# Doubles of the output weights: converted beside the first maxout block instead of beside the experts

## The chip, the cores and the metric

The kernel runs on one core of one Trainium2 chip. The metric is the device time of one execution in microseconds (us). The core's engines are named as the profile names them: PE (matrix products; PEld are its weight loads), DVE (vector), ACT (scalar and activation), POOL, and SP, which here only issues transfers. Each engine takes its instructions in the order in which the program lists them.

## The reference

Three parts follow each other: a linear attention with a norm per head, a mixture of 8 experts (each of 2304 tokens goes to one of them), and a maxout layer with an output product.

```python
kv = einsum('bhsd,bhse->bhde', k, v); out = einsum('bhsd,bhde->bhse', q, kv)
x = out / sqrt(mean(out*out) + 1e-6) * g_norm          # 2304 tokens x 512
e = argmax(x @ w_gate)                                 # one of 8 experts per token, gate weight g
y = g * (maximum(x @ w1[e], 0) @ w2[e])                # w1 512x1024, w2 1024x512 per expert
h = maximum(maximum(y @ m1, y @ m2), y @ m3)           # m1, m2, m3: 512x768
result = h @ w_out                                     # w_out: 768x512
```

The four weights of the last two lines come as 64-bit doubles (`m2w1` to `m2w3` and `m2wo` in the kernel). The gate weight is applied after the output product.

## The kernel before

**Precision.** The engines have no 64-bit type, so a double is first made a float32, from its two 32-bit words: two activations scale the high and the low word (L912, L913), DVE shifts and masks (L914, L915, L917), POOL multiplies and adds (L918, L919). Each float32 weight is then split into a high and a low half that PE takes in its fast format: ACT copies the high half (L297), DVE subtracts for the low half (L298). Every product is three matmuls: high by high, high by low, low by high (`mm3`, L764 to L767).

**Stages.** The attention comes first (to about 88 us), then 8 experts (to about 337 us), then 6 maxout blocks of 384 tokens.

**Experts.** Expert r has an f loop of 8 steps (`gemm1_f`: 12 matmuls into ph, then h by ACT L788 and DVE L789) and a dc loop of 4 steps (`gemm2_dc`: 24 matmuls py, then y by ACT L801). The weights are one expert ahead: `split_next` makes tiles out of raw buffers (four of them, 512 KB each, loaded by SP), one tile per step of the f loop and two per step of the dc loop. In the same steps stand the rounds over the doubles: `DBL1[r]` lists the steps f, `DBL2[r]` the number per step dc. A round (`dbl_step`) stores what was converted three rounds ago to a DRAM tensor (a DMA issued by ACT, L924), loads a block three rounds ahead (SP, L899) and converts a block of 128x256 doubles. There are 48 of these: 36 for the three maxout weights, 12 for the output weights. The float32 results are read back from DRAM as raw buffers (L267, L270) and split.

**Maxout blocks.** Block j has 6 steps c. Each has 36 matmuls into three psum tiles pa (one per weight, out of six psum buffers), then ACT copies the first to m (L1096), DVE takes the maximum with the second and the third (L1097, L1098), ACT and DVE split the result into h2 (L1099, L1100). In block 0 a `split_next(2)` stands between the matmuls of a step and L1096. Then three groups of 18 matmuls pz (L1109 to L1111) form the output of 128 tokens each, over c = 0 to 5, and POOL scatters it by token number.

**What sets the order.** The schedule is manual: each engine's queue holds its instructions in the order of the program. So what is written ahead of L1096 is also ahead of it in ACT's queue. `spill` runs only if an expert has more tokens than its budget.

Of the kernel before, what the change touches and what calls it, by code (L numbers as in the profile page):

```python
# [9 lines left out]
F32 = mybir.dt.float32  # L10
F32R = mybir.dt.float32r
BF16 = mybir.dt.bfloat16
I32 = mybir.dt.int32
U32 = mybir.dt.uint32
ALU = mybir.AluOpType
AF = mybir.ActivationFunctionType
# [5 lines left out]
B, H, S, D = 4, 8, 576, 64  # L22
NT, DM, NE, FF, F2 = B * S, H * D, 8, 1024, 768
NDC, NFC, NC2 = DM // 128, FF // 128, F2 // 128
# [16 lines left out]
def kernel(  # L41
# [16 lines left out]
    nc = tc.nc  # L58
# [3 lines left out]
    xs = dram.tile([ZROW + 1, DM], I32, name="xs")  # L62
    ct = dram.tile([NT, 3], F32, name="ct")

    doubles = []
    if m2w1.dtype == mybir.dt.int64:
        d64 = [m2w1, m2w2, m2w3, m2wo]
        m2w1, m2w2, m2w3 = (dram.tile([DM, F2], F32, name=f"m2w{a}") for a in range(3))
        m2wo = dram.tile([F2, DM], F32, name="m2wo")
        for cb in range(F2 // 256):  # L70
            for a, dst in enumerate([m2w1, m2w2, m2w3]):
                for rb in range(NDC):
                    doubles.append((d64[a], dst, rb, cb))
        for rb in range(NC2):
            for cb in range(DM // 256):
                doubles.append((d64[3], m2wo, rb, cb))
    ND = len(doubles)
    m2w = [m2w1, m2w2, m2w3]

# [151 lines left out]


    sp, act = ENG.SP, ENG.Activation
    NRAW = NE * 8 + 12
    NW = 20
    NT1 = 16 * NE
    e_reg, raws, wt, wpools = {}, {}, {}, {}
# [2 lines left out]
    def wtile(i):  # L240
        if i < NT1:
            s = i % NW
        else:
            s = (i - NT1 + NT1 % NW) % NW if i - NT1 < NW else NW + i - NT1 - NW
        pool = wpools[0 if s < 4 else 1 if s < NW else 2]
        return pool.tile([128, 2, 4, 128], F32R, tag=f"w{s}", name=f"w{i}")

    def raw_dma(i):
        raw = rawp.tile([128, 1024], F32, tag="raw", name=f"raw{i}")
        raws[i] = raw  # L250
        if i < NE * 8:
            r, j = divmod(i, 8)
            if r not in e_reg:
                e_reg[r] = nc.values_load(er_i[0:1, r:r + 1] if r else e0_i[0:1, 0:1], engines=[sp],
                                          min_val=0, max_val=NE - 1)
            e = e_reg[r]
            if j < 4:
                src = w1[ds(e, 1), :, j * 256:(j + 1) * 256].rearrange("o (c p) f -> p (o c) f", p=128)
            else:
                dp_, hf = divmod(j - 4, 2)  # L260
                src = w2[ds(e, 1), hf * 512:(hf + 1) * 512, dp_ * 256:(dp_ + 1) * 256].rearrange(
                    "o (c p) f -> p (o c) f", p=128)
            return nc.sync.dma_start(raw.rearrange("p (c f) -> p c f", c=4), src)
        j = i - NE * 8
        if j < 9:
            a, cp = j % 3, j // 3
            return nc.sync.dma_start(raw.rearrange("p (c f) -> p c f", c=4),  # L267
                                     m2w[a][:, cp * 256:(cp + 1) * 256].rearrange("(c p) f -> p c f", p=128))
        j -= 9
        return nc.sync.dma_start(raw.rearrange("p (c f) -> p c f", c=2),  # L270
                                 m2wo[j * 256:(j + 1) * 256, :].rearrange("(c p) f -> p c f", p=128))

    stream, issued, ready = [0], [0], [8]

# [3 lines left out]
            raw_dma(issued[0])  # L278
            issued[0] += 1

    def split_next(n=1, eng=None):
        for _ in range(n):
            i, half = divmod(stream[0], 2)
            stream[0] += 1
            if i >= NRAW:
                continue
            raw = raws[i]
            t_ = wtile(2 * i + half)
            wt[2 * i + half] = t_
            if i < NE * 8 + 9:  # L290
                src = raw.rearrange("p (c f) -> p c f", c=4)[:, :, half * 128:(half + 1) * 128]
                hi, lo = t_[:, 0], t_[:, 1]
            else:
                src = raw[:, half * 512:(half + 1) * 512]
                hi = t_[:, 0].rearrange("p c f -> p (c f)")
                lo = t_[:, 1].rearrange("p c f -> p (c f)")
            nc.scalar.activation(out=hi, in_=src, func=AF.Copy)  # L297
            (eng or nc.vector).tensor_tensor(out=lo, in0=src, in1=hi.bitcast(F32), op=ALU.subtract)  # L298
            if half == 1:
                raw_upto(i + 5)  # L300

# [598 lines left out]
                              src[rb * 128:(rb + 1) * 128, cb * 256:(cb + 1) * 256].bitcast(I32))  # L900

    def dbl_round(i):

        if i < ND:
            t_ = dt_[i]
            w_ = dpool[0].tile([128, 256], F32, tag="dw", bufs=6, name=f"dw{i}")
            dt_[i, "w"] = w_
            lo, hi = t_[:, :, 0], t_[:, :, 1]  # L910
            wi = w_.bitcast(I32)
            nc.scalar.activation(out=w_, in_=hi.bitcast(F32), func=AF.Copy, scale=2.0 ** -112)  # L912
            nc.scalar.activation(out=lo.bitcast(F32), in_=lo.bitcast(U32), func=AF.Copy, scale=2.0 ** -52)  # L913
            nc.vector.tensor_scalar(out=wi, in0=wi, scalar1=3, scalar2=None, op0=ALU.logical_shift_left)  # L914
            nc.vector.scalar_tensor_tensor(out=wi, in0=hi, scalar=-2 ** 31, in1=wi,  # L915
                                           op0=ALU.bitwise_and, op1=ALU.bitwise_or)
            nc.vector.tensor_scalar(out=hi, in0=wi, scalar1=-2 ** 23, scalar2=None, op0=ALU.bitwise_and)  # L917
            nc.gpsimd.tensor_tensor(out=lo.bitcast(F32), in0=hi.bitcast(F32), in1=lo.bitcast(F32), op=ALU.mult)  # L918
            nc.gpsimd.tensor_tensor(out=w_, in0=lo.bitcast(F32), in1=w_, op=ALU.add)  # L919

    def dbl_store(i):
        if 0 <= i < ND:
# [103 lines left out]
    ct_gen, rk_gen = ct_compute(), ranking()  # L1026


    DBL1 = [(), (3, 5), (3, 5), (1, 3, 5), (1, 4), (1, 4), (1, 4), (1, 3, 5, 7)]
    DBL2 = [(0, 0, 0, 0), (1, 1, 1, 2), (1, 2, 1, 2), (1, 2, 1, 2), (1, 1, 1, 2)] + [(1, 1, 1, 1)] * 2 + [(2, 2, 0, 0)]  # L1030
    for r in range(NE):
        if r == 0:
            parts = [(0, RB[0], slice(0, RB[0]))]
# [48 lines left out]
    for j in range(NYB):  # L1082
        h2 = []
        for c in range(NC2):
            pa = [ps_tile(f"pa{j}{c}{a}") for a in range(3)]
            for a in range(3):
                w_ = m2t(a, c)
                for dc in range(NDC):
                    x_ = ysp[j, dc]
                    mm3(pa[a][:, :YB], w_[:, 0, dc], w_[:, 1, dc], x_[:, 0], x_[:, 1], dc == 0, dc == NDC - 1)  # L1090
            if j == 0:
                split_next(2)
            m_ = xgp.tile([128, H, D], F32, tag="xn", name=f"m{j}{c}").rearrange("p h d -> p (h d)")[:, :YB]
            t_ = hpool.tile([128, 2, YB], F32R, tag="h", name=f"g{j}{c}")
            h2.append(t_)
            nc.scalar.activation(out=m_, in_=pa[0][:, :YB], func=AF.Copy)  # L1096
            nc.vector.tensor_tensor(out=m_, in0=pa[1][:, :YB], in1=m_, op=ALU.max)  # L1097
            nc.vector.tensor_tensor(out=m_, in0=pa[2][:, :YB], in1=m_, op=ALU.max)  # L1098
            nc.scalar.activation(out=t_[:, 0], in_=m_, func=AF.Copy)  # L1099
            nc.vector.tensor_tensor(out=t_[:, 1], in0=m_, in1=t_[:, 0].bitcast(F32), op=ALU.subtract)  # L1100
        if j + 1 < NYB:
            ysplit(j + 1)
        for g in range(NG):
            jt = j * NG + g
            po = ps_tile(f"pz{jt}")
            for c in range(NC2):
                w_ = wot(c).rearrange("p s c f -> p s (c f)")
                h_ = h2[c][:, :, g * 128:(g + 1) * 128]
                nc.tensor.matmul(po, h_[:, 0], w_[:, 0], start=c == 0, stop=False)  # L1109
                nc.tensor.matmul(po, h_[:, 0], w_[:, 1], start=False, stop=False)  # L1110
                nc.tensor.matmul(po, h_[:, 1], w_[:, 0], start=False, stop=c == NC2 - 1)  # L1111
            o_ = xgp.tile([128, H, D], F32, tag="xn", name=f"o{jt}").rearrange("p h d -> p (h d)")
            nc.scalar.activation(out=o_, in_=po, func=AF.Copy, scale=ctab[:, jt, 1:2])  # L1113
            nc.gpsimd.indirect_dma_start(  # L1114
                out=out, out_offset=IndirectOffsetOnAxis(ap=ctab[:, jt, 0:1].bitcast(I32), axis=0),
                in_=o_, in_offset=None)
# [4 lines left out]
    with tc.If(flag):  # L1121
        spill(ctx, tc, dict(
            er_f=er_f, nr_f=nr_f, mr_f=mr_f, trir=trir, capf=capf, e2304=e2304, slot=slot, ident=ident, g2=g2,
            xs=xs, ct=ct, w1=w1, w2=w2, m2w=m2w, m2wo=m2wo, out=out))


def spill(ctx, tc, a):
# [3 lines left out]
    with ExitStack() as st:  # L1131
# [57 lines left out]
        for i in range(3):  # L1189
            nc.sync.dma_start(m2[i], a["m2w"][i].rearrange("(c p) f -> p c f", p=128))  # L1190
        wo = wpool.tile([128, NC2, DM], F32, name="sp_wo")
        nc.sync.dma_start(wo, a["m2wo"].rearrange("(c p) f -> p c f", p=128))

        def ps(nm):
            return psp.tile([128, 512], F32, tag="ps", name=nm)
# [100 lines left out]
```

## Time and profile before

| | before |
|---|---|
| time, median of 3 runs | 647.64 us (646.8 to 650.21) |
| profiled execution, own time | 650.49 us |
| its span (first to last instruction) | 648.6 us |
| mean granted clock of PE | 0.982 |
| PE busy | 619.0 us, 95% of the span |
| DVE busy | 338.0 us, 52% |
| ACT busy | 274.0 us, 42% |
| POOL busy | 196.5 us, 30% |
| bytes moved by DMA | 88.35 MB |

Busy times are unions of the instructions' spans, from one profiled execution, while the median comes from other runs. A busy share over the whole span mixes stages with different limits, so it has to be asked by stage. Matmuls overlap each other, so a busy PE is told best by the distance between the starts of two matmuls. In the rows, "idle before <-releaser" is the time that an engine stood and the instruction that ended it; "w<-raw" reads as "writes w, reads raw".

### The profile page before, as it was taken

Reading aid. Unit: us, or ns where it says so; the run is one execution under the profiler, and the core shown is the slowest. Engines: PE = TensorE matmul, PEld = TensorE weight load, DVE = VectorE, ACT = ScalarE, POOL = GpSimd, SP = SyncE. Lnnn points to the kernel's source line nnn. Section 1 sums busy time; section 2 is a strip of 40 time slices with the busy share of each in tenths; the row PEclk is TensorE's granted clock in tenths of the full one; section 3 lists DMA queues with packets and bytes.
Section 4 is the critical chain, followed back from the end, with each engine's and each line's share of the span. In section 5 each row is a group of like instructions: output and inputs, shape, how many; then the busy total and the mean of one; then the engine's idle time right before and its main releaser. Section 6 shows DMA issues by size and latency. Waiting matters only on the chain.

```text
span 648.6 us, 11278 instructions
## 1 busy us (share of the span) xinstructions
PE 619.0 (95%) x4113; PEld 593.8 (92%) x4113; DVE 338.0 (52%) x718; ACT 274.0 (42%) x629; POOL 196.5 (30%) x278
## 2 busy tenths in 40 slices
PE   8898988999999999999999999999999999999992
PEld 8788888999998989999999989989989989989992
DVE  2546867886889888888985322222322222221220
ACT  1655864856575857576753221121121121121110
POOL 3247643122858585857530010010010010001001
PEclk9978998999999999999999999999999999999997
DMA  8999347866888788888962000000000000000000
GB/s 226 282 297 297 122 164 236 256 234 214 246 249 276 235 264 254 259 251 255 275 184 65 1 34 16 1 33 17 1 33 17 0 17 33 0 17 33 1 18 35
DMA packets 81373, 88.35 MB, mean 136 GB/s; under 512 B 15017, under 2 KB 70825, under 8 KB 81314
## 3 DMA queue, kind: packets, MB, share of 16 engines
q1 hardware_dynamic: 68448, 66.64, 35.5%
q0 software_dynamic: 5952, 14.65, 6.5%
q10 hardware_dynamic: 6914, 6.30, 2.8%
q8 instruction: 34, 0.56, 0.4%
q14 instruction: 25, 0.20, 0.1%
HBM read 71.80 MB, written 15.76 MB: 135 GB/s over the span
## 4 chain that ended last, share of the span: by engine, by line
PE 63%; DVE 9%; DMA 4%; issue 3%; ACT 2%; ACTq 0%; POOL 0%; SPq 0%; DVEq 0%; POOLq 0%
PE pa L767 12%; PE pa L766 12%; PE pa L765 12%; PE py L766 4%; DVE w L298 4%; PE py L767 4%; PE py L765 4%; PE pz L1110 4%; PE pz L1109 4%; PE pz L1111 4%; DVE h L789 2%; DMA d<-in_moe_w_dram 2%; PE ph L767 2%; PE ph L766 2%; PE ph L765 2%
## 5 line engine op out<-in xcount | busy, mean ns | idle before, releaser
L766 PE MATMUL pa<-ys,w 128*128 128x384 f32 x432 | 144.3, 334 | 0.0
L765 PE MATMUL pa<-ys,w 128*128 128x384 f32 x432 | 144.3, 334 | 0.0
L767 PE MATMUL pa<-ys,w 128*128 128x384 f32 x432 | 144.3, 334 | 0.0
L298 DVE TENSOR_TENSOR w<-raw,w 128x512 fp32r<-128x512 f32 x152 | 114.6, 783 | 26.7 <-ACT w L297 23.1
L1114 POOL DMA_INDIRECT out_dram<-o,ctab x18 | 17.5, 973 | 286.9 <-ACT o L1113 276.7
L1097 DVE TENSOR_TENSOR m<-pa,m 128x384 f32<-128x384 f32 x36 | 20.1, 558 | 137.6 <-PE pa L767 137.6
L297 ACT ACTIVATE w<-raw 128x512 fp32r<-128x512 f32 x152 | 89.5, 624 | 4.8 <-DMA raw<-in_moe_w_dram 4.8
L766 PE MATMUL py<-h,w 128*128 128x324 f32 (+7 forms) x256 | 81.4, 318 | 7.2 <-DVE h L789 7.2
L1099 ACT ACTIVATE g<-m 128x384 fp32r<-128x384 f32 x36 | 18.9, 526 | 150.0 <-DVE m L1098 150.0
L766 PEld LDWEIGHTS pa<-ys,w 128*128 128x128 f32 x432 | 81.1, 188 | 0.2
L765 PEld LDWEIGHTS pa<-ys,w 128*128 128x128 f32 x432 | 81.1, 188 | 0.2
L767 PEld LDWEIGHTS pa<-ys,w 128*128 128x128 f32 x432 | 81.1, 188 | 0.0
L765 PE MATMUL py<-h,w 128*128 128x324 f32 (+7 forms) x256 | 80.2, 313 | 0.0
L767 PE MATMUL ph<-xt,w 128*128 128x324 f32 (+7 forms) x256 | 79.6, 311 | 0.5 <-DVE w L298 0.5
L765 PE MATMUL ph<-xt,w 128*128 128x324 f32 (+7 forms) x256 | 79.3, 310 | 0.6 <-ACT xt L667 0.6
L767 PE MATMUL py<-h,w 128*128 128x324 f32 (+7 forms) x256 | 79.8, 312 | 0.0
L766 PE MATMUL ph<-xt,w 128*128 128x324 f32 (+7 forms) x256 | 79.4, 310 | 0.2 <-DVE xt L668 0.2
L766 PEld LDWEIGHTS py<-h,w 128*128 128x128 f32 x256 | 48.8, 191 | 10.8 <-DVE h L789 10.6
L918 POOL TENSOR_TENSOR d<-d 128x256 f32<-128x256 f32 x48 | 30.7, 640 | 75.5 <-issue 18.2
L765 PEld LDWEIGHTS ph<-xt,w 128*128 128x128 f32 x256 | 48.3, 189 | 0.8 <-ACT xt L667 0.8
L767 PEld LDWEIGHTS ph<-xt,w 128*128 128x128 f32 x256 | 48.3, 189 | 0.8 <-DVE w L298 0.8
L765 PEld LDWEIGHTS py<-h,w 128*128 128x128 f32 x256 | 48.9, 191 | 0.0
(247 smaller groups left out, 1034.1 us busy)
## 6 DMA issues: line engine op xcount, KB each, us to landing
raw<-in_moe_w_dram SPq DMA_DIRECT2D x64, 512.0 KB, 5.4
d<-in_moe_w_dram SPq DMA_DIRECT2D x36, 256.0 KB, 5.2
m2w<-dw ACTq DMA_DIRECT2D x36, 128.0 KB, 4.5
raw<-m2w SPq DMA_DIRECT2D x9, 512.0 KB, 4.6
k<-in_k_dram SPq DMA_DIRECT2D x8, 512.0 KB, 8.7
v<-in_v_dram SPq DMA_DIRECT2D x8, 512.0 KB, 9.2
q<-in_q_dram SPq DMA_DIRECT2D x8, 512.0 KB, 8.5
d<-in_moe_w_out_dram SPq DMA_DIRECT2D x12, 256.0 KB, 5.2
```

The source lines that it names most:

```text
L297: nc.scalar.activation(out=hi, in_=src, func=AF.Copy)
L298: (eng or nc.vector).tensor_tensor(out=lo, in0=src, in1=hi.bitcast(F32), op=ALU.subtract)
L765: nc.tensor.matmul(po, lhi, rhi, start=first, stop=False)
L766: nc.tensor.matmul(po, lhi, rlo, start=False, stop=False)
L767: nc.tensor.matmul(po, llo, rhi, start=False, stop=last)
L918: nc.gpsimd.tensor_tensor(out=lo.bitcast(F32), in0=hi.bitcast(F32), in1=lo.bitcast(F32), op=ALU.mult)
L1097: nc.vector.tensor_tensor(out=m_, in0=pa[1][:, :YB], in1=m_, op=ALU.max)
L1099: nc.scalar.activation(out=t_[:, 0], in_=m_, func=AF.Copy)
L1109: nc.tensor.matmul(po, h_[:, 0], w_[:, 0], start=c == 0, stop=False)
L1110: nc.tensor.matmul(po, h_[:, 0], w_[:, 1], start=False, stop=False)
L1111: nc.tensor.matmul(po, h_[:, 1], w_[:, 0], start=False, stop=c == NC2 - 1)
L1114: nc.gpsimd.indirect_dma_start(out=out, out_offset=IndirectOffsetOnAxis(ap=ctab[:, jt, 0:1].bitcast(I32), axis=0), in_=o_, in_offset=None)
```

## The change

Only the 36 blocks of the three maxout weights stay in the rounds beside the experts. Their places in `DBL1` and `DBL2` are set anew: expert 1 to 7 had 7, 8, 9, 7, 6, 6 and 8 steps, and has 7, 8, 8, 6, 4, 3 and 3 (the last three steps only store). The output weights are loaded as doubles into the raw buffers (128 rows, 512 KB each, six of them), and `split_next` converts them in block 0 of the maxout stage, 128x512 at a time, into a tile of the pool from which m and the outputs come (tag xn, three buffers), and splits that into the weight tile. Step c = 0 still splits two tiles of a maxout weight; c = 1 converts two tiles, c = 2 to 5 one each. Both halves of each tile are also stored to DRAM (`m2wos`, 512 KB per tile, on SP's queue), where `spill` would read them. Gone are the float32 copy of the output weights in DRAM, its 12 stores and its three reloads. The conversion's seven instructions are the same, moved into a function.

```diff
-        d64 = [m2w1, m2w2, m2w3, m2wo]
+        d64 = [m2w1, m2w2, m2w3]
-        m2wo = dram.tile([F2, DM], F32, name="m2wo")
+        m2wos = dram.tile([F2, 2, DM], F32, name="m2wos")
-        for rb in range(NC2):
-            for cb in range(DM // 256):
-                doubles.append((d64[3], m2wo, rb, cb))
...
-    NRAW = NE * 8 + 12
+    NRAW = NE * 8 + 9 + NC2
...
-        return nc.sync.dma_start(raw.rearrange("p (c f) -> p c f", c=2),
-                                 m2wo[j * 256:(j + 1) * 256, :].rearrange("(c p) f -> p c f", p=128))
+        return nc.sync.dma_start(raw.bitcast(I32), m2wo[j * 128:(j + 1) * 128, :].bitcast(I32))
...
+    def to_float32(lo, hi, w_):
+        wi = w_.bitcast(I32)
+        nc.scalar.activation(out=w_, in_=hi.bitcast(F32), func=AF.Copy, scale=2.0 ** -112)
+        nc.scalar.activation(out=lo.bitcast(F32), in_=lo.bitcast(U32), func=AF.Copy, scale=2.0 ** -52)
+        nc.vector.tensor_scalar(out=wi, in0=wi, scalar1=3, scalar2=None, op0=ALU.logical_shift_left)
+        nc.vector.scalar_tensor_tensor(out=wi, in0=hi, scalar=-2 ** 31, in1=wi,
+                                       op0=ALU.bitwise_and, op1=ALU.bitwise_or)
+        nc.vector.tensor_scalar(out=hi, in0=wi, scalar1=-2 ** 23, scalar2=None, op0=ALU.bitwise_and)
+        nc.gpsimd.tensor_tensor(out=lo.bitcast(F32), in0=hi.bitcast(F32), in1=lo.bitcast(F32), op=ALU.mult)
+        nc.gpsimd.tensor_tensor(out=w_, in0=lo.bitcast(F32), in1=w_, op=ALU.add)
...
             else:
-                src = raw[:, half * 512:(half + 1) * 512]
-                hi = t_[:, 0].rearrange("p c f -> p (c f)")
-                lo = t_[:, 1].rearrange("p c f -> p (c f)")
+                half = 1
+                hi, lo = (t_[:, x].rearrange("p c f -> p (c f)") for x in range(2))
+                src = xgs[0].tile([128, H, D], F32, tag="xn", name=f"wd{i}").rearrange("p h d -> p (h d)")
+                words = raw.bitcast(I32).rearrange("p (f c) -> p f c", c=2)
+                to_float32(words[:, :, 0], words[:, :, 1], src)
             nc.scalar.activation(out=hi, in_=src, func=AF.Copy)
-            (eng or nc.vector).tensor_tensor(out=lo, in0=src, in1=hi.bitcast(F32), op=ALU.subtract)
+            nc.vector.tensor_tensor(out=lo, in0=src, in1=hi.bitcast(F32), op=ALU.subtract)
+            if i >= NE * 8 + 9:
+                c0 = (i - NE * 8 - 9) * 128
+                nc.sync.dma_start(m2wos[c0:c0 + 128].rearrange("p s f -> p (s f)"),
+                                  t_.bitcast(F32).rearrange("p s c f -> p (s c f)"))
             if half == 1:
                 raw_upto(i + 5)
...
-    DBL1 = [(), (3, 5), (3, 5), (1, 3, 5), (1, 4), (1, 4), (1, 4), (1, 3, 5, 7)]
-    DBL2 = [(0, 0, 0, 0), (1, 1, 1, 2), (1, 2, 1, 2), (1, 2, 1, 2), (1, 1, 1, 2)] + [(1, 1, 1, 1)] * 2 + [(2, 2, 0, 0)]
+    DBL1 = [(), (3, 5, 7), (1, 3, 5, 7), (1, 3, 5, 7), (3, 7), (7,), (), (1, 3, 5)]
+    DBL2 = [(0,) * 4] + [(1,) * 4] * 3 + [(1,) * 4, (1, 1, 1, 0), (1, 1, 1, 0), (0,) * 4]
...
             if j == 0:
-                split_next(2)
+                split_next(2 if c < 2 else 1)
```

## Rows read from the trace of the kernel before

**Rows 1.** Busy by stage: us, then PE, PEld, DVE, ACT, POOL, PEclk, DMA, GB/s.
```profile
215.00:245.00 30.00, 28.72 (x195) 27.95 (x193) 27.35 (x51) 19.67 (x47) 20.30 (x27) 1.00 0.81 253
337.00:387.00 50.00, 50.00 (x272) 47.65 (x272) 20.01 (x36) 15.81 (x32) 1.99 (x2) 1.00 0.10 33
```

**Rows 2.** PE's waits: waiting line, releaser, us in total, times, longest.
```profile
PE py L766 <- DVE h L789: 7.2, 13, 1.2
```

**Rows 3.** Timeline of PE, experts 0 and 7: start, us, instruction [idle before <-releaser].
```profile
107.81 0.42 PE L766 MATMUL py<-h,w 128*128 128x324 f32 x1 [1.16 <-DVE h L789]
...
109.42 0.54 PE L766 MATMUL py<-h,w 128*128 128x324 f32 x1 [0.90 <-DVE h L789]
...
325.21 0.30 PE L767 MATMUL py<-h,w 128*128 128x284 f32 x1
325.35 0.29 PE L765 MATMUL py<-h,w 128*128 128x284 f32 x1
325.83 0.40 PE L766 MATMUL py<-h,w 128*128 128x284 f32 x1 [0.19 <-DVE h L789]
326.07 0.29 PE L767 MATMUL py<-h,w 128*128 128x284 f32 x1
```

**Rows 4.** Timeline of ACT, DVE and POOL: one conversion of 128x256 doubles, expert 1.
```profile
134.83 0.44 ACT L912 ACTIVATE dw<-d 128x256 f32<-128x256 f32 x1 [1.78 <-DMA d<-in_moe_w_dram]
...
135.79 0.29 DVE L914 TENSOR_SCALAR dw<-dw 128x256 int32<-128x256 int32 x1
136.11 0.43 DVE L915 SCALAR_TENSOR_TENSOR dw<-d,dw 128x256 int32<-128x256 int32 x1
136.57 0.30 DVE L917 TENSOR_SCALAR d<-dw 128x256 int32<-128x256 int32 x1
...
137.01 0.61 POOL L918 TENSOR_TENSOR d<-d 128x256 f32<-128x256 f32 x1 [12.94 <-DVE d L917]
137.70 1.07 POOL L919 TENSOR_TENSOR dw<-d,dw 128x256 f32<-128x256 f32 x1
```

**Rows 5.** Instructions by line: duration ns min/median/max, first and last start, forms.
```profile
L297 ACT ACTIVATE w<-raw x152: 613/623/650, 84.5 to 357.6; 128x512 fp32r<-128x512 f32 x152
L298 DVE TENSOR_TENSOR w<-raw,w x152: 675/691/1441, 85.2 to 358.3; 128x512 fp32r<-128x512 f32 x152
L516 POOL TENSOR_TENSOR orow<-ohl,rnorm x15: 1031/1034/1343, 28.9 to 68.1; 128x512 f32<-128x512 f32 x12, 64x512 f32<-64x512 f32 x3
L919 POOL TENSOR_TENSOR dw<-d,dw x48: 739/1064/1114, 137.7 to 333.6; 128x256 f32<-128x256 f32 x48
```

**Rows 6.** Timeline of ACT and DVE in maxout block 0, c = 1 and 2.
```profile
344.56 1.14 ACT L297 ACTIVATE w<-raw 128x512 fp32r<-128x512 f32 x2
345.62 0.49 ACT L1096 ACTIVATE m<-pa 128x384 f32<-128x384 f32 x1
350.38 0.53 ACT L1099 ACTIVATE g<-m 128x384 fp32r<-128x384 f32 x1 [4.26 <-DVE m L1098]
350.81 1.13 ACT L297 ACTIVATE w<-raw 128x512 fp32r<-128x512 f32 x2
351.86 0.49 ACT L1096 ACTIVATE m<-pa 128x384 f32<-128x384 f32 x1
...
350.94 0.56 DVE L1100 TENSOR_TENSOR g<-m,g 128x384 fp32r<-128x384 f32 x1 [0.59 <-ACT g L1099]
```

**Rows 7.** Timeline of PE: first and sixteenth matmul of the first pz group.
```profile
374.55 0.39 PE L1109 MATMUL pz<-w,g 128*128 128x512 f32 x1
...
378.03 0.40 PE L1109 MATMUL pz<-w,g 128*128 128x512 f32 x1
```

**Rows 8.** DMA issues of the page: queue, count, KB each, us to landing.
```profile
raw<-in_moe_w_dram SPq DMA_DIRECT2D x64, 512.0 KB, 5.4
```

**Rows 9.** Busy by stretch around expert 0's waits; columns as in rows 1.
```profile
106.20:109.60 3.40, 1.34 (x7) 0.81 (x7) 3.40 (x7) 0.51 (x2) 0.00 (x0) 0.99 0.70 211
109.60:113.00 3.40, 3.40 (x14) 3.40 (x15) 0.17 (x1) 1.35 (x5) 0.00 (x0) 0.50 0.96 284
```

More of the change, by code (lines that the diff above doesn't have):

```diff
@@ L279, in raw_upto, with split_next @@
             issued[0] += 1
-    def split_next(n=1, eng=None):
+    def to_float32(lo, hi, w_):
[8 more added lines that the diff above has]
+        nc.gpsimd.tensor_tensor(out=w_, in0=lo.bitcast(F32), in1=w_, op=ALU.add)
+    def split_next(n=1):
         for _ in range(n):
-            i, half = divmod(stream[0], 2)
+            t = stream[0]
             stream[0] += 1
-            if i >= NRAW:
+            if t >= NT1 + 18 + NC2:
                 continue
+            i = t // 2 if t < NT1 + 18 else NE * 8 + 9 + t - NT1 - 18
             raw = raws[i]
-            t_ = wtile(2 * i + half)
-            wt[2 * i + half] = t_
+            t_ = wtile(t)
+            wt[t] = t_
             if i < NE * 8 + 9:
+                half = t % 2
                 src = raw.rearrange("p (c f) -> p c f", c=4)[:, :, half * 128:(half + 1) * 128]
@@ L909, in dbl_round @@
             dt_[i, "w"] = w_
[L910 to L919, printed above, removed]
+            to_float32(t_[:, :, 0], t_[:, :, 1], w_)
     def dbl_store(i):
@@ L1123 @@
             er_f=er_f, nr_f=nr_f, mr_f=mr_f, trir=trir, capf=capf, e2304=e2304, slot=slot, ident=ident, g2=g2,
-            xs=xs, ct=ct, w1=w1, w2=w2, m2w=m2w, m2wo=m2wo, out=out))
+            xs=xs, ct=ct, w1=w1, w2=w2, m2w=m2w, m2wos=m2wos, out=out))
 def spill(ctx, tc, a):
@@ L1191, in spill @@
         wo = wpool.tile([128, NC2, DM], F32, name="sp_wo")
-        nc.sync.dma_start(wo, a["m2wo"].rearrange("(c p) f -> p c f", p=128))
+        wl = wpool.tile([128, NC2, DM], F32, name="sp_wl")
+        for i, w_ in enumerate((wo, wl)):
+            nc.sync.dma_start(w_, a["m2wos"].rearrange("(c p) s f -> s p c f", p=128)[i])
+        V.tensor_tensor(out=wo, in0=wo, in1=wl, op=ALU.add)
         def ps(nm):
```

## The prediction, made before the result was known

> **What bounds the kernel now.** I read the busy times by stage first, then PE's own waits, then the order on ACT and DVE around the first maxout block.
>
> By stage there are two kinds of work [rows 1]. In the first maxout block PE is busy for all of its 50 us, while DVE works 20 us, ACT 16 us and POOL 2 us: PE is the bound, and the others have room. In the experts PE and DVE are nearly level: in a stretch of expert 4, DVE is busy 27.35 us of 30 and PE 28.72.
>
> PE's waits say what the experts lose. Thirteen times PE stood before a py matmul until DVE had written an h, 7.2 us in all [rows 2]. Two of these are in expert 0, which holds no double in either kernel: 1.16 and 0.90 us [rows 3]. Eleven, 5.1 us, are in experts 1 to 7: one in expert 1, none in expert 2, the rest in 3 to 7. A wait costs more than its idle time, because the pipeline fills again: around 325.83 two starts lie 0.48 and then 0.24 us apart against 0.14 between undisturbed ones (325.21 to 325.35) [rows 3]. That is 0.34 + 0.10 us for an idle of 0.19, so about 0.25 us on top of each. Eleven waits then cost 5.1 + 11 x 0.25 = 7.9 us. No change to the doubles can give back more than this in the experts.
>
> **Part 1: twelve conversions leave the experts.** Rounds per expert 1 to 7 were 7, 8, 9, 7, 6, 6, 5 and become 7, 8, 8, 6, 4, 3, 0. Each round holds 0.29 + 0.43 + 0.30 us of DVE [rows 4], and lengthens what DVE does beside POOL's two instructions. With each go two activations, a 256 KB load on SP's queue, a 128 KB store issued by ACT, and for all together three 512 KB reloads on SP's queue; these ran beside PE, and I give them no price of their own. The six splits into tiles stay.
>
> Where PE waited, DVE was late with the last h of an expert, so I count rounds that stand before it. Expert 1: unchanged before the last h, its wait (about 0.6 us with refill) stays. Expert 2: one round more in its f loop, but the last step of expert 1 holds one round instead of two, so I take 0 to 0.3 us of new wait. Expert 3: the same three in the loop, one less just before it: half of its loss stays, about 0.6. Expert 4 has two less before its last h, 5 and 6 two or more less, 7 none at all: their losses go. Left are about 1.4 us, so the gain is 6.5. Bounds: 7.9 if all goes, 3 if expert 2 takes over expert 3's wait and half of the others stay.
>
> **Part 2: six conversions of 128x512 enter the first maxout block.** PE's rows c follow each other, and per c ACT and DVE do: splits for c, the copy m of pa[0] (L1096), two maxima (L1097, L1098), the split of h (L1099, L1100). Now the splits of c = 1 (two) and c = 2 to 5 (one each) become a conversion, and they stand ahead of m in ACT's order. ACT, after its two scalings, must issue the tile's high half, which waits for POOL's sum. All else of ACT for this c is queued behind this wait, and DVE's maxima wait for ACT's copy. So the conversion is no longer beside the maxout work but in series with it.
>
> Length L from the first scaling to the start of the high half. No row shows it at 128x512. At 128x256 one ran almost undisturbed from 134.83 to 138.77, 3.94 us [rows 4]. Doubling the width costs ACT 0.44 to 0.62 us [rows 4, 5] and DVE 0.43 to 0.69 [rows 4, 5], a factor of 1.4 to 1.6. So: scaling 0.62; DVE 0.29, 0.43, 0.30 become 0.46, 0.69, 0.48; POOL's product 0.61 becomes 1.15 (1.03 is the row of another POOL product of 128x512, 1.22 twice the row); POOL's sum, 0.74 to 1.11 at 128x256, was slow where DVE ran beside it, and DVE now stands idle, so 1.35; hand-offs between engines 0.43, mostly the 0.14 ahead of POOL and 0.1 on either side of DVE [rows 4]. Sum: L = 5.2 us. Bounds: 3.9 (nothing longer than at half the width) and 6.7 (all durations doubled). I take 5.2, near the rows of full width.
>
> The Trainium skill (GPSIMD Engine Reference, section 3.1) gives 4497 ns for a two-input add of 2048 fp32 elements; a quarter would be 1.12 us for each POOL step, an estimate from that page, and L would be 5.0 with it. No run so far shows the step at this width.
>
> From the high half on: 0.52 us later ACT is free; the low half (0.60) delays the first maximum to 1.25, then 0.59 for each maximum, so L1099 starts at 2.43, and the next scaling 0.43 after it (350.38 to 350.81), the h ready 1.12 after it (350.38 to 351.50) [rows 6]. The next scaling is thus 2.86, the h 3.55 us behind the high half. Chain: the first scaling can start at 344.56 [rows 6]; two conversions for c = 1 with 0.52 between, four more with 2.86 before each: 344.56 + 0.52 + 4 x 2.86 + 6L + 3.55 = 360.07 + 6L. With L = 5.2 the last h of the block is ready at 391.3. PE needs it for the sixteenth pz matmul, before at 378.03 [rows 7]. PE's own work cannot hide this: per c it is 6.24 us (m at 345.62 and 351.86 [rows 6]) against L + 2.86 = 8.1 for the chain, and with six psum buffers, three per c, PE runs two c ahead at most and then waits. Loss: 391.3 - 378.0 = 13.2 us; by the bounds 5.4 and 22.2.
>
> The raw loads are 512 KB each, as before for the other weights, and land in 5.4 us [rows 8]. On SP's queue a raw load for c = 4 now stands behind the 512 KB store of the first tile, which waits for that tile's low half; it is wanted 16 us later, in c = 4, so I price it at nothing, and if that cover were gone at 5.4 us. The six stores (3 MB) are read by no later work unless tokens spill.
>
> **Clock.** PE's granted clock falls after waits: in 106.2 to 109.6 PE was busy 1.34 of 3.4 us, and the next 3.4 us were granted at 0.50, that is at 1.2 instead of 2.4 GHz [rows 9]. Ahead of the last h of the block PE would stand about 7 us (the h before it is ready L + 2.86 earlier, and only 0.7 us of pz can follow on that). Half clock for 3.4 us of full work costs 1.7 us; for twice that 3.4. I take 2, bounds 0 and 5.
>
> **Sum.** -6.5 + 13.2 + 2 = +8.7 us. The profiled execution took 650.49 us for a span of 648.6, so it would take 659.2; it lies 2.85 above the median of the runs, 647.64, from which the forecast is 656.3, 1.3% more.
>
> **Rivals.** (1) Hidden: PE does not slow, the six psum buffers carry it, and only the experts' gain remains. Place: ACT's queue in the first block; price: L. With L at 3.0 the last h comes at 378 and the time is 647.6 - 6.5 = 641; break-even, with no loss of clock, is L = 4.1. For: the other engines have 30 us of room there [rows 1]. Against: the work at half the width already took 3.94 us [rows 4]. (2) The experts don't pay: the added round in expert 2 makes it wait as expert 3 did, the loads stay late, and the gain is 0 to 2: 661 to 663. For: DVE is full there [rows 1]. Against: the rounds of experts 4 to 7, where most of that time is lost, fall from 24 to 13. (3) The clock: PE, waiting 2 us in each c, is granted half speed through the block. Then PE itself is the bound: four c at 12.5 us and 54 pz at 0.46 (twice 6.24 and twice the 0.23 of [rows 7]), from 349.6, where the first two c end, reach 424.6 instead of 387.1, the sum is +31 and the time 679. For: a fall followed waits in [rows 9]. Against: there PE stood for 2 of 3.4 us, here for a quarter of the time until the last wait. The Trainium skill's TensorE: Matmul & The Clock Gate (A second HAM failure mode: psum-queue depth-cycling) tells of this case, a clock that swings between its two levels because PE pauses between groups for psum; no row of this trace shows it in the maxout stage. (4) The change does not do what it says: only with weights that are not doubles, but the trace has doubles loaded.
>
> **Chances.** Forecast 0.72, (1) 0.12, (2) 0.12, (3) 0.04. Range: low from L near 4.5 with the full gain of 7.9 and no clock loss, 647.6 + 9.0 - 7.9 = 648.7, and part of (1) below it is left out, so 649; high from L = 6.2, clock 4, gain 4: 647.6 + 19.2 = 667, with (2) inside. A run can tell about 0.5%, 3.2 us: faster than that only in half of (1), 0.06; within it the other half and the lowest edge of the forecast, 0.08; slower 0.86.
>
> **What would show it.** Right: per c of the first block ACT waits some 3 to 4 us for POOL in the middle of a split, the rows m (L1096) lie about 8 us apart instead of 6.24, PE has waits before pa and one long one inside the first pz, and the second block starts 13 to 16 us later after the start of the first; PE's waits before py in experts 4 to 7 are gone. Wrong: m rows 6.24 us apart (rival 1), or the experts' waits as before (rival 2), or a granted clock of 0.5 over most of the block (rival 3). Most of all the forecast hangs on L, six times in the sum: each 0.5 us of it is 3 us.

## The result, and the profile after

The changed kernel took 652.54 us (median of 19 runs), the kernel before in the same comparison 648.04: a ratio of 1.0083, 95% interval 1.0061 to 1.0105. That is 5.4 us slower, where 8.7 were forecast. The ratio and its interval are formed from the fast runs and are not the quotient of the two medians, which is 1.0069, or 4.5 us.

The profiled execution of the changed kernel took 650.15 us for a span of 648.5, as long as that of the kernel before (648.6). This does not contradict the ratio: expert 1 began at 117.25 us in it and at 123.69 in the profile before, but at 116.84 in a second profile of the kernel before (e7_before_again below, on another chip). The time ahead of expert 1 thus differs between executions of one kernel by more than the change is worth, so the profiles are compared stage by stage and not by their spans.

Busy by stage of the kernel after: the first row is experts 2 to 7, the second the first maxout block, then three stretches around its last wait (us, then PE, PEld, DVE, ACT, POOL, PEclk, DMA, GB/s).

```profile
152.58:324.06 171.48, 171.48 (x1213) 171.45 (x1213) 137.62 (x263) 110.02 (x252) 96.23 (x123) 1.00 0.79 236
324.06:386.88 62.82, 52.78 (x272) 48.43 (x271) 27.31 (x50) 21.54 (x41) 16.02 (x14) 0.95 0.28 101
...
369.20:372.60 3.40, 1.03 (x5) 0.50 (x3) 1.41 (x3) 0.40 (x1) 1.71 (x2) 0.99 0.00 0
372.60:376.00 3.40, 0.00 (x0) 0.00 (x0) 1.72 (x3) 1.25 (x3) 0.61 (x1) 0.50 0.17 72
376.00:379.40 3.40, 3.06 (x7) 2.48 (x8) 2.43 (x5) 2.62 (x6) 0.35 (x1) 0.50 0.21 84
```

The same stages of the kernel before, cut at the same matmuls (the first ph of expert 2, the first pa of block 0, the first pa of block 1):

```profile
158.00:337.09 179.09, 174.22 (x1213) 171.66 (x1213) 155.88 (x300) 116.82 (x275) 117.11 (x149) 1.00 0.84 253
337.09:387.08 49.99, 49.99 (x272) 47.60 (x271) 19.92 (x36) 15.81 (x32) 1.99 (x2) 1.00 0.10 32
```

Experts 2 to 7 became 7.6 us shorter, and PE is now busy for all of their 171.48 us. Block 0 became 12.8 us longer, with PE busy 52.8 of 62.8 us, where it was busy throughout [rows 1]. The rest, from block 1 to the end, is the same to 0.1 us.

PE's waits after (waiting line, releaser, us in total, times, longest; L784 and L785 are the former L765 and L766, L808 the former L789, L1106 the former L1099, L1103 the former L1096, L1116 the former L1109):

```profile
PE pz L1116 <- ACT g L1106: 6.1, 1, 6.1
PE py L785 <- DVE h L808: 3.0, 4, 1.2
...
PE pa L784 <- ACT m L1103: 2.6, 2, 1.3
...
PE pz L1116 <- ACT m L1103: 1.3, 1, 1.3
```

Of the thirteen waits for an h [rows 2] four are left, two in expert 0 and two in expert 1. New are three waits for the copy m and one of 6.1 us for the last h of the block.

The order in step c = 2 of block 0 after the change, ACT, then DVE, then POOL (start, us, instruction; L283 and L284 are the scalings, L285 to L288 the shift and masks, L289 and L290 product and sum, L312 the high half):

```profile
344.86 0.65 ACT L283 ACTIVATE wd<-raw 128x512 f32<-128x512 f32 x1
345.42 0.67 ACT L284 ACTIVATE raw<-raw 128x512 f32<-128x512 uint32 x1
349.74 0.63 ACT L312 ACTIVATE w<-wd 128x512 fp32r<-128x512 f32 x1 [3.65 <-POOL wd L290]
350.27 0.47 ACT L1103 ACTIVATE m<-pa 128x384 f32<-128x384 f32 x1
352.26 0.53 ACT L1106 ACTIVATE g<-m 128x384 fp32r<-128x384 f32 x1 [1.51 <-DVE m L1105]
352.69 0.66 ACT L283 ACTIVATE wd<-raw 128x512 f32<-128x512 f32 x1
...
345.54 0.43 DVE L285 TENSOR_SCALAR wd<-wd 128x512 int32<-128x512 int32 x1
346.00 0.69 DVE L286 SCALAR_TENSOR_TENSOR wd<-raw,wd 128x512 int32<-128x512 int32 x1
346.73 0.43 DVE L288 TENSOR_SCALAR raw<-wd 128x512 int32<-128x512 int32 x1
...
347.29 1.04 POOL L289 TENSOR_TENSOR raw<-raw 128x512 f32<-128x512 f32 x1 [5.41 <-DVE raw L288]
348.41 1.30 POOL L290 TENSOR_TENSOR wd<-raw,wd 128x512 f32<-128x512 f32 x1
```

ACT stands 3.65 us before the high half, with the copy m behind it in its queue. From the first scaling to the high half, the L of the prediction, are 349.74 - 344.86 = 4.88 us (4.91 for the first conversion of the block); the next scaling follows 2.95 us later, so a step takes 7.83 us, against the 6.24 that PE needs for it. Before, the copy m began 1.05 us after the splits of its step (350.81 to 351.86 [rows 6]).

At the end of the block PE waits for the chain, and then runs at half clock (timeline of PE after):

```profile
376.34 0.79 PE L1116 MATMUL pz<-w,g 128*128 128x512 f32 x1 [6.10 <-ACT g L1106]
376.93 0.63 PE L1117 MATMUL pz<-w,g 128*128 128x512 f32 x1
377.36 0.63 PE L1118 MATMUL pz<-w,g 128*128 128x512 f32 x1
```

The sixteenth pz matmul starts 52.28 us after the first pa (324.06 to 376.34), before 40.94 (337.09 to 378.03 [rows 7]): 11.3 us of chain. From there to the next block are 10.54 us instead of 9.05: 1.5 us of half clock and refill. The pz starts lie 0.43 us apart until about 379, not 0.23.

### The profile page after: what moved, and what is told of

Its sections match the earlier page's. It is cut to its first block, busy times and chain, and to the rows that moved or that the text cites. A ratio compares the mean times of both kernels' runs of the same rounds, so it can differ in the third digit from the quotient of the medians.

```text
span 648.5 us, 11170 instructions
## 1 busy us (share of the span) xinstructions
PE 613.7 (95%) x4113; PEld 588.7 (91%) x4113; DVE 329.5 (51%) x700; ACT 272.6 (42%) x617; POOL 192.6 (30%) x266
## 3 DMA queue, kind: packets, MB, share of 16 engines
q1 hardware_dynamic: 67632, 68.21, 35.6%
## 5 line engine op out<-in xcount | busy, mean ns | idle before, releaser
L784 PE MATMUL pa<-ys,w 128*128 128x384 f32 x432 | 144.7, 335 | 2.6 <-ACT m L1103 2.6
L785 PE MATMUL pa<-ys,w 128*128 128x384 f32 x432 | 144.3, 334 | 0.0
L313 DVE TENSOR_TENSOR w<-raw,w 128x512 fp32r<-128x512 f32 x146 | 107.2, 762 | 31.7 <-ACT w L312 28.5
L312 ACT ACTIVATE w<-raw 128x512 fp32r<-128x512 f32 x146 | 86.1, 624 | 5.9 <-DMA raw<-in_moe_w_dram 5.9
L784 PEld LDWEIGHTS pa<-ys,w 128*128 128x128 f32 x432 | 81.1, 188 | 3.8 <-ACT m L1103 3.6
L785 PE MATMUL py<-h,w 128*128 128x324 f32 (+7 forms) x256 | 80.3, 314 | 3.1 <-DVE h L808 3.0
L785 PEld LDWEIGHTS pa<-ys,w 128*128 128x128 f32 x432 | 81.1, 188 | 0.2
L784 PE MATMUL py<-h,w 128*128 128x324 f32 (+7 forms) x256 | 80.2, 313 | 0.0
L784 PE MATMUL ph<-xt,w 128*128 128x324 f32 (+7 forms) x256 | 79.3, 310 | 0.6 <-ACT xt L686 0.6
L785 PE MATMUL ph<-xt,w 128*128 128x324 f32 (+7 forms) x256 | 79.2, 309 | 0.2 <-DVE xt L687 0.2
L1106 ACT ACTIVATE g<-m 128x384 fp32r<-128x384 f32 x36 | 18.9, 525 | 137.7 <-DVE m L1105 137.7
L785 PEld LDWEIGHTS py<-h,w 128*128 128x128 f32 x256 | 48.9, 191 | 4.5 <-DVE h L808 4.2
L1116 PE MATMUL pz<-w,g 128*128 128x512 f32 x108 | 43.5, 403 | 7.4 <-ACT g L1106 6.1
L784 PEld LDWEIGHTS ph<-xt,w 128*128 128x128 f32 x256 | 48.1, 188 | 0.8 <-ACT xt L686 0.8
```

The source lines that it names most:

```text
L313: nc.vector.tensor_tensor(out=lo, in0=src, in1=hi.bitcast(F32), op=ALU.subtract)
L784: nc.tensor.matmul(po, lhi, rhi, start=first, stop=False)
L785: nc.tensor.matmul(po, lhi, rlo, start=False, stop=False)
```

## The experiments

The theory under test: the block is longer because ACT waits inside a conversion while the copy of pa stands behind it, and the twelve rounds taken from the experts are what made these shorter. The main rival: the conversions cost the block their work, in whatever order. The first four kernels ran on one chip, the last three on another. Each is compared with the kernel before on its own chip, whose median was 656.59 us on the first and 649.34 on the second. The times in the expectations start from 648.04 for the kernel before, so they are compared as ratios to it.

| run | time, us | ratio to before (95%) | experts 2 to 7, us | block 0, us |
|---|---|---|---|---|
| e1_apart | 647.9 | 0.9883 (0.9846 to 0.9920) | 172.09 | 49.98 |
| e2_no_conversion | 646.36 | 0.9851 (0.9818 to 0.9883) | 171.48 | 49.98 |
| e3_experts_as_before | 670.96 | 1.0226 (1.0196 to 1.0256) | 180.62 | 63.37 |
| e4_dve_sums | 654.88 | 0.9990 (0.9955 to 1.0025) | 172.14 | 57.84 |
| e5_rounds_moved | 636.47 | 0.9819 (0.9785 to 0.9852) | 171.48 | 49.98 |
| e6_changed_again | 652.47 | 1.0054 (1.0023 to 1.0084) | 171.48 | 63.14 |
| e7_before_again | 646.41 (one run) | | 179.02 | 50.01 |

**e1_apart: the conversion of a tile one step ahead of its split.**

```diff
...
+    wd = {}
+
+    def convert(t):
+        i = NE * 8 + 9 + t - NT1 - 18
+        wd[t] = xgs[0].tile([128, H, D], F32, tag="xn", name=f"wd{i}").rearrange("p h d -> p (h d)")
+        words = raws[i].bitcast(I32).rearrange("p (f c) -> p f c", c=2)
+        to_float32(words[:, :, 0], words[:, :, 1], wd[t])
...
-                src = xgs[0].tile([128, H, D], F32, tag="xn", name=f"wd{i}").rearrange("p h d -> p (h d)")
-                words = raw.bitcast(I32).rearrange("p (f c) -> p f c", c=2)
-                to_float32(words[:, :, 0], words[:, :, 1], src)
+                src = wd[t]
...
             if j == 0:
-                split_next(2 if c < 2 else 1)
+                split_next(1 if c else 2)
+                convert(NT1 + 18 + c)
...
+        if j == 0:
+            split_next(1)
         if j + 1 < NYB:
             ysplit(j + 1)
```

> Same conversions in the same block, but the conversion of tile c+1 is issued in step c and its split into halves one step later, so that ACT never stands before POOL's sum. Theory (series: the block is longer only because ACT waits inside a conversion with the copy of pa behind it): block 0 is back at 50.0 us, the experts keep their 6.6 us, the time is 641.5 us, 1.0% faster than before. Rival (work: the six conversions and their stores cost the block time by themselves, through DVE, POOL or DMA, in whatever order): block 0 stays at 55 us or more, the time at 647 to 652.

Its stages (experts 2 to 7, block 0):

```profile
163.02:335.11 172.09, 171.84 (x1214) 171.53 (x1213) 137.99 (x263) 110.00 (x252) 95.43 (x123) 1.00 0.76 235
335.11:385.09 49.98, 49.98 (x273) 47.58 (x271) 27.07 (x50) 20.99 (x41) 16.14 (x14) 1.00 0.33 124
```

One step of its block 0, ACT and then POOL (L318 is the high half of the tile converted a step earlier, L1110 the copy m, L1113 the high half of h):

```profile
348.38 0.53 ACT L1113 ACTIVATE g<-m 128x384 fp32r<-128x384 f32 x1 [3.32 <-DVE m L1112]
348.81 0.62 ACT L318 ACTIVATE w<-wd 128x512 fp32r<-128x512 f32 x1
349.33 0.66 ACT L283 ACTIVATE wd<-raw 128x512 f32<-128x512 f32 x1
349.89 0.67 ACT L284 ACTIVATE raw<-raw 128x512 f32<-128x512 uint32 x1
350.45 0.48 ACT L1110 ACTIVATE m<-pa 128x384 f32<-128x384 f32 x1
354.62 0.53 ACT L1113 ACTIVATE g<-m 128x384 fp32r<-128x384 f32 x1 [3.69 <-DVE m L1112]
...
351.81 1.04 POOL L289 TENSOR_TENSOR raw<-raw 128x512 f32<-128x512 f32 x1 [3.46 <-DVE raw L288]
352.94 1.31 POOL L290 TENSOR_TENSOR wd<-raw,wd 128x512 f32<-128x512 f32 x1
```

The work is all there (DVE 27.1 us in the block, POOL 16.1, as in the changed kernel), but the copy m no longer waits for POOL: POOL works at 351.81 to 354.25, while ACT has long passed it. A step takes 6.24 us again, the block 49.98. The rival of the work (647 to 652, a ratio of 0.998 or more) falls, and the kernel is 1.2% faster than before. The expected 641.5 is a ratio of 0.990, inside the interval.

**e2_no_conversion: block 0 without the conversion.**

```diff
-                src = xgs[0].tile([128, H, D], F32, tag="xn", name=f"wd{i}").rearrange("p h d -> p (h d)")
-                words = raw.bitcast(I32).rearrange("p (f c) -> p f c", c=2)
-                to_float32(words[:, :, 0], words[:, :, 1], src)
-            nc.scalar.activation(out=hi, in_=src, func=AF.Copy)
+                src = hi.bitcast(F32)
+                nc.scalar.activation(out=hi, in_=raw.bitcast(U32)[:, 0:512], func=AF.Copy, scale=2.0 ** -36)
+            if i < NE * 8 + 9:
+                nc.scalar.activation(out=hi, in_=src, func=AF.Copy)
```

This kernel leaves out the conversion: one scaling makes the high half straight from a word of each double, so the output weights are not the right ones, while loads, splits into halves and stores stay.

> The changed kernel without the conversion in block 0: the high half is made straight from one word of the doubles, so the output weights are wrong; loads, splits and stores stay. Theory (series): block 0 at 50.0 us, the experts 6.6 us shorter than before, 641.5 us. Rival (the experts' gain is chance of one profile, or comes from the front of the kernel): 648, as before. If the stores or loads of block 0 cost PE time: block 0 over 51.

```profile
164.26:335.74 171.48, 171.48 (x1213) 171.45 (x1213) 138.03 (x263) 109.98 (x252) 96.70 (x123) 1.00 0.77 236
335.74:385.72 49.98, 49.98 (x272) 47.59 (x271) 18.34 (x32) 14.57 (x29) 1.99 (x2) 1.00 0.35 125
```

The stages are those of e1_apart (experts 2 to 7 within 0.6 us), and the intervals of the two ratios overlap: with the order of e1_apart the conversion costs no time that these runs can tell. The 512 KB loads and stores, which stay, cost block 0 nothing: 49.98 us. Both stages came out as expected, yet the ratio lies below the expected 0.990, also by its interval; what is left lies outside these two stages, where executions of one kernel differ too, and its cause stays open.

**e3_experts_as_before: the old rounds and the new block together.**

```diff
-        d64 = [m2w1, m2w2, m2w3]
+        d64 = [m2w1, m2w2, m2w3, m2wo]
...
+        m2wx = dram.tile([F2, DM], F32, name="m2wx")
+        for rb in range(NC2):
+            for cb in range(DM // 256):
+                doubles.append((d64[3], m2wx, rb, cb))
...
+    DBL1 = [(), (3, 5), (3, 5), (1, 3, 5), (1, 4), (1, 4), (1, 4), (1, 3, 5, 7)]
+    DBL2 = [(0, 0, 0, 0), (1, 1, 1, 2), (1, 2, 1, 2), (1, 2, 1, 2), (1, 1, 1, 2)] + [(1, 1, 1, 1)] * 2 + [(2, 2, 0, 0)]
```

> Block 0 as in the changed kernel, but beside the experts all 48 conversions with the old places (the twelve of the output weights go to a tensor that nothing reads). Theory (series, and the two parts add up): block 0 at 62.8 us, the experts as before, the time 648.0 + 12.8 = 661. Rival (the gain in the experts is not from the twelve rounds): 652 to 655.

```profile
164.90:345.52 180.62, 175.69 (x1214) 173.36 (x1213) 155.70 (x300) 117.04 (x275) 117.05 (x149) 0.99 0.83 252
345.52:408.89 63.37, 53.20 (x273) 48.75 (x272) 29.01 (x54) 22.93 (x44) 16.08 (x14) 0.95 0.28 102
```

Both parts come back, each in its place: the experts at 180.6 us, the block at 63.4. Against the first profile of the kernel before these are 1.5 and 13.4 us more, 14.9 together, and the ratio of 1.0226 is 14.8 us on this chip (expected: 661, a ratio of 1.020, inside the interval). The experts' gain is thus from the twelve rounds and the places of all of them; this run changes both at once and does not tell them apart.

**e4_dve_sums: POOL's product and sum on DVE, only in block 0.**

```diff
...
-        nc.gpsimd.tensor_tensor(out=lo.bitcast(F32), in0=hi.bitcast(F32), in1=lo.bitcast(F32), op=ALU.mult)
-        nc.gpsimd.tensor_tensor(out=w_, in0=lo.bitcast(F32), in1=w_, op=ALU.add)
+        eng.tensor_tensor(out=lo.bitcast(F32), in0=hi.bitcast(F32), in1=lo.bitcast(F32), op=ALU.mult)
+        eng.tensor_tensor(out=w_, in0=lo.bitcast(F32), in1=w_, op=ALU.add)
```

The call in block 0 passes DVE as `eng`, the call beside the experts POOL.

> In block 0 POOL's product and sum run on DVE, the order is unchanged. Theory (series, L counted six times): two steps of 0.69 in place of 1.04 and 1.31 and one hand-off less bring L from 4.91 to about 3.75, the last h comes 6 x 1.15 = 6.9 us sooner, block 0 takes about 55 us (with less or no loss of clock), the time 645. Rival (work): DVE has 8 us more to do in the block, so the time is 652 or more.

ACT and DVE of a conversion and PE's first matmul after its last wait, then the block and the stretches around that wait:

```profile
352.52 0.66 ACT L283 ACTIVATE wd<-raw 128x512 f32<-128x512 f32 x1
...
356.39 0.63 ACT L312 ACTIVATE w<-wd 128x512 fp32r<-128x512 f32 x1 [2.64 <-DVE wd L290]
...
354.93 0.69 DVE L289 TENSOR_TENSOR raw<-raw 128x512 f32<-128x512 f32 x1
355.66 0.69 DVE L290 TENSOR_TENSOR wd<-raw,wd 128x512 f32<-128x512 f32 x1
...
380.00 0.79 PE L1116 MATMUL pz<-w,g 128*128 128x512 f32 x1 [5.10 <-ACT g L1106]
```

```profile
333.78:391.62 57.84, 52.74 (x273) 49.29 (x272) 35.64 (x62) 21.58 (x41) 2.00 (x2) 0.94 0.30 110
...
380.00:383.50 3.50, 3.50 (x8) 2.81 (x9) 2.42 (x5) 2.29 (x5) 0.79 (x1) 0.50 0.11 42
383.50:392.00 8.50, 8.50 (x35) 6.84 (x34) 0.00 (x0) 0.88 (x2) 1.21 (x2) 0.89 0.17 64
```

L is 3.87 us, 1.0 shorter (expected 3.75), and the sixteenth pz matmul starts 46.2 us after the first pa instead of 52.3: 6.1 us for six times 1.0. More work for DVE (35.6 us in the block instead of 27.3) made the block shorter, which the rival excludes; its 652, a ratio of 1.006, lies above the interval. The expected block of 55 us (57.84 measured) and time of 645 (a ratio of 0.995, just outside the interval) were both missed: besides the longer L, part of the gain went to the clock, which stayed at half longer after PE had begun again (0.89 over the 8.5 us from 383.5 means half for 1.9 of them, so to about 385.4), so that the rest of the block took 11.6 us instead of 9.05. The loss by half clock and refill is thus 1.5 us in one kernel and 2.6 in the other, though PE's wait was shorter in the second (5.1 against 6.1 us).

**e5_rounds_moved: e1_apart with the 36 rounds placed anew.** Expert 1 was left with waits in e1_apart, and experts 4 to 7 had room.

```diff
-    DBL1 = [(), (3, 5, 7), (1, 3, 5, 7), (1, 3, 5, 7), (3, 7), (7,), (), (1, 3, 5)]
-    DBL2 = [(0,) * 4] + [(1,) * 4] * 3 + [(1,) * 4, (1, 1, 1, 0), (1, 1, 1, 0), (0,) * 4]
+    DBL1 = [(), (7,), (3, 5, 7), (3, 5, 7), (3, 7), (3, 7), (7,), (1, 2, 4, 5)]
+    DBL2 = [(0,) * 4, (1, 1, 1, 0)] + [(1,) * 4] * 5 + [(0,) * 4]
```

> The kernel of e1_apart with the 36 rounds placed anew: expert 1 holds none before its last h (4 in all instead of 7), experts 4 to 7 take them (6, 6, 5 and 4 steps). Theory (expert 1 waits because rounds stand on DVE before its last h while their doubles land late; experts 4 to 7 have room): PE's waits before py in expert 1, about 4 us of idle and refill in e1_apart, go, experts 2 to 7 keep 172 us, and the time falls 2 to 4 us below e1_apart, ratio to before about 0.983 to 0.985. Rival (expert 1 is late through its own weights' loads and the table load): expert 1 stays within 1 us of e1_apart and the ratio at 0.988. Rival (experts 4 to 7 wait again when their rounds come back): experts 2 to 7 take 174 us or more.

Its stages: expert 1, experts 2 to 7, block 0; then expert 1 of e1_apart.

```profile
119.81:154.41 34.60, 34.08 (x207) 33.63 (x206) 27.51 (x72) 22.34 (x50) 5.03 (x8) 1.00 0.73 237
154.41:325.89 171.48, 171.48 (x1214) 171.45 (x1213) 135.06 (x269) 111.17 (x256) 100.70 (x127) 1.00 0.79 241
325.89:375.87 49.98, 49.98 (x273) 47.58 (x272) 27.05 (x50) 20.93 (x41) 16.09 (x14) 1.00 0.33 122
```

```profile
124.46:163.02 38.56, 36.06 (x204) 34.89 (x205) 31.59 (x78) 23.75 (x54) 8.36 (x12) 0.96 0.70 234
```

Expert 1 is 4.0 us shorter than in e1_apart, and as much shorter than in e6_changed_again below, which has e1_apart's rounds and ran on the same chip as this kernel; PE's waits there for an h (2 in e1_apart, 3 in e6_changed_again) are gone. Experts 2 to 7 did not wait again. The kernel is 1.8% faster than before, the lowest ratio of the kernels measured here (expected 0.983 to 0.985); its interval just overlaps that of e1_apart, so the step from there is not fully clear of noise.

**e6_changed_again and e7_before_again: the two kernels on another chip.** Neither is edited.

> The changed kernel once more, on the same chip as the others of this call. Theory: block 0 at 62.8 us within 1.5 us (the length of the half clock can differ), experts 2 to 7 at 171.5, ratio to before 1.006 to 1.010, also on a chip on which all kernels are slower.

> The kernel before, with a profile from the same chip as the others of this call. Theory: experts 2 to 7 at 179.1 us and block 0 at 50.0 as in its first profile, since nothing in them depends on the front of the kernel; what differs between chips lies in the attention and in experts 0 and 1.

Expert 1, experts 2 to 7 and block 0 of the changed kernel, then of the kernel before:

```profile
117.21:155.80 38.59, 36.16 (x206) 34.79 (x205) 31.44 (x78) 23.27 (x54) 9.06 (x12) 0.96 0.71 233
155.80:327.28 171.48, 171.48 (x1213) 171.45 (x1213) 137.67 (x263) 110.09 (x252) 97.05 (x123) 1.00 0.77 236
327.28:390.42 63.14, 53.07 (x272) 48.66 (x271) 27.30 (x50) 21.52 (x41) 16.06 (x14) 0.95 0.28 100
```

```profile
116.84:154.04 37.20, 34.92 (x205) 33.58 (x206) 29.63 (x75) 22.96 (x52) 6.50 (x9) 1.00 0.71 228
154.04:333.06 179.02, 174.21 (x1214) 171.60 (x1213) 155.86 (x300) 116.81 (x275) 117.47 (x149) 1.00 0.83 253
333.06:383.07 50.01, 50.01 (x273) 47.62 (x271) 19.91 (x36) 15.81 (x32) 2.00 (x2) 1.00 0.10 37
```

In experts 2 to 7 and in block 0 both kernels repeat their first profiles to 0.4 us. The ratio, 1.0054, lies a little lower than the first, with overlapping intervals, and just below the 1.006 that was expected. What varies is expert 1 and the time ahead of it.

## Why the prediction was right

The place, the mechanism and the direction were right, and the sum was 3 us too high. Of the signs that it named, ACT's wait of 3 to 4 us inside each conversion (3.65), the copies m about 8 us apart (7.83), PE's waits before pa and the long one inside pz all came, and the waits of experts 4 to 7 went; the second block started 12.8 us later after the first, just short of the 13 to 16 named.

| term | forecast, us | measured, us |
|---|---|---|
| experts 2 to 7 (forecast with expert 1) | -6.5 | -7.6 (179.09 to 171.48) |
| expert 1 | 0 | +1.0 in the first pair of profiles |
| chain in block 0 | +13.2 | +11.3 |
| half clock (and refill) after the last wait | +2 | +1.5 |
| sum | +8.7 | +6.2 in these stages, +5.4 by the ratio of the runs |

- **Experts.** The bound from PE's waits [rows 2, 3], 7.9 us for experts 1 to 7 with about 0.6 of it in expert 1, left 7.3 for experts 2 to 7, and 7.6 came back. PE stood 4.87 us there before (179.09 - 174.22), so its ten waits cost 0.27 us each on top, where I had 0.25. I left about 0.8 us of waiting in experts 2 and 3; the kernel after has none there. From expert 2's last h to its own, expert 3 has eight rounds in DVE's queue instead of nine. Before, PE waited twice for it (timeline of PE before):

```profile
208.21 0.42 PE L766 MATMUL py<-h,w 128*128 128x330 f32 x1 [0.51 <-DVE h L789]
...
209.98 0.42 PE L766 MATMUL py<-h,w 128*128 128x330 f32 x1 [1.05 <-DVE h L789]
```

I had expected half of this to stay.

- **Expert 1.** I called it unchanged. It took 34.31 us before and 35.33 after in the first profiles, 37.20 and 38.59 in the second pair, but 38.9 in e3_experts_as_before, which has the old places. Whether the new places cost it 1 us or this is spread stays open. In e5_rounds_moved, which holds no round ahead of expert 1's last h, PE does not wait for an h there; but the kernel before, with its rounds, took 34.31 us in one profile, less than the 34.60 of e5_rounds_moved, so what such rounds cost differs from execution to execution.
- **Chain.** The form 360.07 + 6L was good, its L was the mis-sized term: 4.91 us, not 5.2. The DVE steps came out at 0.43, 0.69, 0.43 (forecast 0.46, 0.69, 0.48), POOL's at 1.04 and 1.31 (1.15, 1.35), and the hand-offs at 0.34, not 0.43. Six times 0.29 is 1.7 us. No row before had a conversion of this width, and L = 5.2 was added up from scaled parts, most of them a little too long. I also let PE wait for both halves of the last h, but it begins with the high half, which is ready 3.1 us behind the tile's high half, not 3.55; against that a step ran 2.95, not 2.86, behind it. Together -1.8 of 13.2, which is what was measured.
- **The estimate from a page.** The Trainium skill's figure (GPSIMD Engine Reference, section 3.1) gave an estimate of 1.12 us per POOL step; the trace shows 1.04 and 1.31, so its sum, 2.24 against 2.35, was nearer than mine of 2.50. With it the terms of L add up to 4.9 us, not to the 5.0 that I wrote, and 4.9 is what was measured, though in part by chance, since neither step alone took 1.12.
- **Clock.** Forecast 2, measured with the refill 1.5 here and 2.6 in e4_dve_sums. The wait ahead of the last h was 6.1 us, not 7.
- **Rivals.** Hidden work (1) is excluded by the waits in block 0. It is what e1_apart has: the room was there [rows 1], and the order kept the kernel from it. The experts that don't pay (2) are excluded by their 171.48 us, measured here, in e2_no_conversion and in e6_changed_again, and by e3_experts_as_before. The clock that swings through the block (3), as the Trainium skill's TensorE: Matmul & The Clock Gate (A second HAM failure mode: psum-queue depth-cycling) tells of it, was not seen: the granted clock fell at 372.6, in the long wait at the block's end, and not at PE's waits of 1.3 us before pa.

## What to carry to other kernels

Work that is moved beside a bound engine can cost its own latency when a queue that feeds this engine waits inside it, however idle the other engines are. Where a moved chain crosses engines (here ACT, DVE, POOL and back to ACT), issue its first part one step ahead of its last, as in e1_apart: the same instructions then went from 12.8 us to nothing. And where an engine is late at a known point, count the work that stands before this point, not the engine's busy share: with eight rounds instead of nine before expert 3's last h its waits of 1.6 us were gone. Other rounds moved with it, so that the one round alone did this is not shown.

## What the runs showed of the hardware that I had not expected

- POOL's two steps of the same shape differ: 1.04 us for the product and 1.31 for the sum, both 128x512 and with DVE idle; on DVE both took 0.69. Whether the operation or the layout of its operands makes the difference was not tried.
- After a wait of 6.1 us PE ran at half clock for 3.1 us more (376.3 to 379.4), after one of 5.1 us for some 5.4 (380.0 to 385.4): the shorter wait cost more. What differs is when the clock fell: at 372.56 in the first, 2.3 us into the wait, so that 3.8 us at half clock passed while PE stood, and at 378.6 in the second (e4_dve_sums), 3.7 us into the wait, so that only 1.4 us did. In e6_changed_again, whose wait was 6.1 us too, the clock was at half from 376.5 to 383.3, 3.7 us of it after PE had begun again at 379.58, and block 0 took 63.14 us instead of 62.82.
